# Two operand sums on VectorE, and a running sum on GpSimd: a change to the opening of a gated-mix kernel

## The chip, the cores and the metric

The kernel runs on one core of one Trainium2 chip. Its time is that of the whole launch, in device microseconds. Five engines work side by side, each with its own queue in program order: TensorE (PE, with its weight loads PEld), VectorE (DVE), ScalarE (ACT), GpSimd (POOL) and SyncE (SP). SyncE and GpSimd also issue DMA transfers, SyncE plain ones and GpSimd those that add to what is there (accumulating loads). Both kinds are moved by the same 16 DMA engines.

## What is computed

For x of 2048 rows and 512 columns:

```
q, k, v = split(x @ wqkv)                      # 32 heads of 16
phi(t)  = where(t > 0, t + 1, exp(t)) + 1e-6
kv = sum over rows of phi(k)^T v ;  z = sum over rows of phi(k)
a  = (phi(q) kv / (phi(q) z + 1e-6)) @ wo
b  = ((x @ w_gate) * (x @ w_up)) @ w_down
g  = sigmoid(sum(x * gate_w))
out = g * a + (1 - g) * b
```

All in float32, with EPS = 1e-6.

## The kernel before

**Three products for one.** TensorE multiplies in a shorter format, so that every float32 operand is split into a high part (a copy by ScalarE, `act`, line 58) and a low part (source less high part, by VectorE, `tt`, line 61). Each product is three matmuls (`mm3`, line 74): high by high, low by high, high by low. `split_late` (line 270) issues the high part at once and puts the low part on a list, `lows`, which `extras` (line 541) empties at the end of the same half step.

**Seven products for eight.** A product of two-by-two blocks is made in seven block products of sums of blocks (Strassen's scheme), numbered 1 to 7. `SUMS` (line 167) says which blocks of x make the operand of each: operand 3 is B1 - B2, 4 is A2 - A1, 1 is A1 + B2, 6 is A1 + B1, 7 is A2 + B2, while 2 is A1 and 5 is B2 alone. They are used in the order `UNIT` = 2, 3, 4, 1, 5, 6, 7.

**The two stages.** The main stage, from about 96 us on, makes q, the gate and up products and w_down. The first stage, which the change is about, makes k and v. It goes in steps of half steps:

- Steps 0 to 3: four lead tiles of 128 rows (tiles 8 to 11), their v by plain products (`plain`, line 299); their k came just before. The lead's x lies in `xa`.
- Steps 4 to 10: couples 4 and 5, seven block products each (s = 0 to 6), one of each couple in a step. Their operands are half-width sums of x (`sub`, lines 401 to 418).
- Steps 11 to 17 and 18 to 24: couples 0 and 1, then 2 and 3, with the full operands `xc` (operand 2 and 7 lie in `xa`, 3 and 5 in `xb`, which the lead and the half-width sums use before; 1, 4 and 6 have tiles of their own).

A product of block i of a couple adds to one of four PSUM banks Y, X, R, S (`couple`, line 429). Between the products `crit` moves results: m2 from Y by ScalarE, R = X - m2 by VectorE (called cR in the profile), v from Y, t, S, and so on. In a step, the first couple's product stands first, then the other couple's `crit`, then the second couple's product and the first couple's `crit`.

**phi and the sums over rows.** `phi_k` (line 302) makes exp and relu on ScalarE, joins them on VectorE, and adds the result and EPS to `zacc` on VectorE (line 307): the sum z. `phi_end` (line 310) adds EPS on ScalarE and frees a tile. `kv_add` multiplies phi(k) and v of a tile into `pkv` by 128 small matmuls; `gkv` gives the steps of the four groups of tiles. `z_sums` (line 611) reads `zacc` in slot 6 of the main stage.

**Operands of couples 0 to 3.** `op_load`, `op_add`, `op_turn` and `op_split` (lines 374 to 423) make them. For operands 2, 1, 5, 6 and 7: load a block into a DRAM scratch `xstage` (SyncE), add the other block there with an accumulating load (GpSimd), bring the sum to the low part's place in SBUF (`op_turn`, SyncE), split. For operands 3 and 4: load a block into two SBUF tiles `xo`, scale by -1 on ScalarE, add the other block with accumulating loads, split. `sub_load` and `sub_add` do the same for the half-width sums, in single `xo` tiles: seven loads at the start, then five accumulating loads.

**What sets the order.** Nothing is reordered: each engine runs its instructions as the program issues them. `plan(step, fn)` (line 334) puts a function at a half step; `AT` (line 40) holds the half steps, in the order of `UNIT` for the names with `gs` and `go`. So `goload` 3 for operand 2 means the second half of step 1. Negative numbers are run ahead of the lead. Within a half step, functions run in the order in which they were planned: phi first, then w_v's splits, then the operands, then the sums of weights and their splits.

**Work tiles.** `get` (line 187) takes the first of a list of 45 tiles, `put` (line 193) adds one at its end. An instruction that writes a tile handed out again waits until the last reader of its former content is done, and with it waits all that stands behind it in its queue.

**Weights of k and v.** w_k and w_v are loaded as four row blocks each (`raw_of`). `sum_make` (line 351) builds the sums of weight blocks on VectorE, `fac_split` (line 361) splits them, `split_v` (line 279) splits w_v's row blocks.

Of the kernel before, what the change touches and what calls it, by code (L numbers as in the profile page):

```python
# [1288 lines left out]
```

## Time and profile before

| What | Value |
| --- | --- |
| Three runs | 592.89, 591.58, 594.45 us (median 592.89) |
| Profiled execution | 593.48 us, its span 591.5 us |
| TensorE busy | 582.2 us (98%) |
| VectorE busy | 505.0 us (85%) |
| ScalarE busy | 418.3 us (71%) |
| GpSimd busy | 67.3 us (11%) |
| Mean granted TensorE clock | 0.996 |
| DMA | 99.29 MB, mean 168 GB/s |

In rows of the timeline the first number is the start in us from the span's beginning, the second the duration, then engine, line, operation, and output<-inputs; in square brackets stands the idle time of the engine just before and what ended it. A DMA row of SPq or POOL is the issue, not the transfer. Tile names are the program's: `xo` is a raw block of x or a sum being built, `xbh` and `xbl` are the high and low part in `xb`, `e` and `ph` belong to phi, `wvl` is w_v's low part, `c` with Y, X, R or S a couple's bank.

### The profile page before, as it was taken

Reading aid. Unit: us, or ns where it says so; the run is one execution under the profiler, and the core shown is the slowest. Engines: PE = TensorE matmul, PEld = TensorE weight load, DVE = VectorE, ACT = ScalarE, POOL = GpSimd, SP = SyncE. Lnnn points to the kernel's source line nnn. Section 1 sums busy time; section 2 is a strip of 40 time slices with the busy share of each in tenths; the row PEclk is TensorE's granted clock in tenths of the full one; section 3 lists DMA queues with packets and bytes.
Section 4 is the critical chain, followed back from the end, with each engine's and each line's share of the span. In section 5 each row is a group of like instructions: output and inputs, shape, how many; then the busy total and the mean of one; then the engine's idle time right before and its main releaser. Section 6 shows DMA issues by size and latency. Waiting matters only on the chain.

```text
span 591.5 us, 8699 instructions
## 1 busy us (share of the span) xinstructions
PE 582.2 (98%) x3047; PEld 474.6 (80%) x3047; DVE 505.0 (85%) x820; ACT 418.3 (71%) x755; POOL 67.3 (11%) x85
## 2 busy tenths in 40 slices
PE   8998999999999999999999999999999999999997
PEld 6785888777888888888888888888888888888885
DVE  7796687889698989998999976969899989889882
ACT  4588577879887878787974574887777677876300
POOL 0332000201111111111001100101101010100000
PEclk9999999999999999999999999999999999999999
DMA  8999674889797889878478356766847574631011
GB/s 280 227 271 235 205 169 148 196 209 222 183 251 178 213 203 242 192 183 212 109 219 218 115 133 188 150 139 149 188 106 162 150 159 116 134 81 35 1 74 69
DMA packets 45884, 99.29 MB, mean 168 GB/s; under 512 B 4384, under 2 KB 16928, under 8 KB 45728
## 3 DMA queue, kind: packets, MB, share of 16 engines
q0 software_dynamic: 11216, 37.49, 36.2%
q1 hardware_dynamic: 34336, 60.91, 30.0%
q8 instruction: 24, 0.39, 0.3%
q10 hardware_dynamic: 288, 0.33, 0.2%
q14 instruction: 20, 0.16, 0.1%
HBM read 87.43 MB, written 16.53 MB: 176 GB/s over the span
## 4 chain that ended last, share of the span: by engine, by line
PE 88%; ACT 4%; DMA 4%; DVE 2%; issue 1%; POOL 0%; SPq 0%; ACTq 0%; POOLq 0%
PE pdn L52 28%; PE bR L52 15%; PE bX L52 14%; PE bY L52 14%; PE bS L52 7%; PE pM L52 3%; DMA xo<-in_xp 2%; PE cR L52 2%; PE cY L52 2%; DMA wraw<-in_wqkv 2%; PE cX L52 1%; ACT e L58 1%; PE cS L52 1%; PE pkv L52 1%; ACT v L58 0%
## 5 line engine op out<-in xcount | busy, mean ns | idle before, releaser
L61 DVE TENSOR_TENSOR wcl<-wr,wch 128x512 fp32r<-128x512 f32 (+1 forms) x96 | 72.7, 772 | 5.2 <-ACT wch L58 5.2
L58 ACT ACTIVATE M<-pdn 128x512 f32<-128x512 f32 x84 | 49.9, 595 | 26.8 <-PE pdn L52 25.0
L52 PE MATMUL pdn<-hl,dh 128*128 128x512 f32 x176 | 68.5, 389 | 0.0
L52 PE MATMUL pdn<-hh,dh 128*128 128x512 f32 x176 | 68.5, 389 | 0.0
L52 PE MATMUL pdn<-hh,dl 128*128 128x512 f32 x176 | 68.5, 389 | 0.0
L58 ACT ACTIVATE wch<-wr 128x512 fp32r<-128x512 f32 (+1 forms) x96 | 66.7, 700 | 1.3 <-DMA wr<-in_wq_add 1.2
L61 DVE TENSOR_TENSOR M<-M,pdn 128x512 f32<-128x512 f32 x75 | 51.0, 681 | 13.9 <-PE pdn L52 13.7
L58 ACT ACTIVATE hh<-c 128x512 fp32r<-128x512 f32 x56 | 35.2, 629 | 37.0 <-DVE c L61 36.8
L85 POOL DMA_DIRECT2D wr<-in_wgu_add x28 | 24.3, 866 | 240.1 <-ACT wr L58 126.9
L52 PE MATMUL bX<-xbh,wch 128*128 128x512 f32 x128 | 49.8, 389 | 0.0
L52 PE MATMUL bX<-xbh,wcl 128*128 128x512 f32 x128 | 49.8, 389 | 0.0
L52 PE MATMUL bX<-xbl,wch 128*128 128x512 f32 x128 | 49.8, 389 | 0.0
L58 ACT ACTIVATE pdn<-M 128x512 f32<-128x512 f32 x61 | 35.9, 589 | 11.7 <-DVE M L61 11.7
L52 PEld LDWEIGHTS pdn<-hh,dh 128*128 128x128 f32 x176 | 33.0, 188 | 7.0
L52 PEld LDWEIGHTS pdn<-hl,dh 128*128 128x128 f32 x176 | 33.0, 188 | 7.0
L61 DVE TENSOR_TENSOR hl<-c,hh 128x512 fp32r<-128x512 f32 x56 | 38.3, 684 | 0.4
L52 PEld LDWEIGHTS pdn<-hh,dl 128*128 128x128 f32 x176 | 33.0, 188 | 6.8
L58 ACT ACTIVATE wr<-wr 128x512 f32<-128x512 f32 x64 | 36.7, 627 | 0.0
L61 DVE TENSOR_TENSOR dl<-dr,dh 128x512 fp32r<-128x512 f32 (+1 forms) x40 | 29.7, 764 | 2.3 <-ACT dh L58 2.1
L58 ACT ACTIVATE c<-bX 128x512 f32<-128x512 f32 x28 | 16.8, 600 | 20.0 <-DVE bS L61 20.0
L58 ACT ACTIVATE m<-bY 128x512 f32<-128x512 f32 x32 | 18.9, 591 | 16.5 <-PE bY L52 16.5
L58 ACT ACTIVATE dh<-dr 128x512 fp32r<-128x512 f32 (+1 forms) x40 | 27.1, 685 | 4.1 <-PE pdn L52 3.4
(265 smaller groups left out, 1597.3 us busy)
## 6 DMA issues: line engine op xcount, KB each, us to landing
wr<-in_wgu_add POOLq DMA_DIRECT2D x28, 640.0 KB, 6.4
wr<-in_wgu SPq DMA_DIRECT2D x28, 384.0 KB
dr<-in_wdn_add POOLq DMA_DIRECT2D x12, 640.0 KB, 6.9
dr<-in_wdn SPq DMA_DIRECT2D x12, 384.0 KB
xraw<-in_x SPq DMA_DIRECT2D x16, 256.0 KB
terms<-zq SPq DMA_DIRECT2D x16, 256.0 KB
zt<-terms SPq DMA_DIRECT2D x16, 256.0 KB
rb<-den SPq DMA_DIRECT2D x16, 256.0 KB
```

The costliest lines, as they stand in the source:

```text
L52: tc.keep_in_program_order(nc.tensor.matmul(*args, **kw))
L58: pin(nc.scalar.activation(dst, src, func, **kw))
L61: pin(nc.vector.tensor_tensor(dst, a, b, op=op))
L85: tc.keep_in_program_order(nc.gpsimd.dma_start(dst, src, accum_op=ALU.add))
```

## The change

Four edits, and new half steps in `AT`:

1. Operands 2 and 5 leave the DRAM scratch. `op_load(4)` now loads the blocks of operands 4 and 2 (A2 and A1), `op_load(3)` those of operands 3 and 5 (B1 and B2), each into four `xo` tiles with plain loads. `op_add` subtracts the one from the other on VectorE; the tiles of A1 and B2 are then split as operands 2 and 5 themselves. The scaling on ScalarE and the accumulating loads of operands 3 and 4 are gone.
2. `zacc` no longer gets phi and EPS from VectorE in `phi_k`; GpSimd adds the finished phi in `phi_end`.
3. In the couples, `phi_end` of all four tiles comes in s = 1 and 2 of the next pair of couples. Before, two of them came at s = 5 and two at s = 0 of the next.
4. The splits of w_v's first two row blocks are planned at -3, ahead of the sums of weights at -1; all four stood behind those sums on VectorE before.

In `AT`, by operand: loads of 4 at half step 5 (was 13), of 3 at 11 (was 9), of 1 at 7 (same), of 6 and 7 at 9 (were 11 and 9); splits of 2 at 11 (13), 3 at 19 (19), 4 at 10 (25), 1 at 23 (25), 5 at 25 (30), 6 at 27 (26), 7 at 28 (30). The last split of a weight sum is at 16 (18), and two groups of kv products come a step later (15 for 14, 28 for 27).

```diff
-'gwsplit': (-1, -1, 7, 9, 11, 13, 12, 14, 15, 18), 'goload': (3, 9, 13, 7, 11, 11, 9), 'goadd': (3, 14, 17, 9, 1, 13, 17), 'gosplit': (13, 19, 25, 25, 30, 26, 30)
+'gwsplit': (-1, -1, 7, 9, 11, 13, 12, 14, 15, 16), 'goload': (0, 11, 5, 7, 0, 9, 9), 'goadd': (0, 14, 8, 9, 0, 12, 14), 'gosplit': (11, 19, 10, 23, 25, 27, 28)
...
-'gkv': (6, 14, 22, 27)
+'gkv': (6, 15, 22, 28)
...
-'goturn': (7, 1, 5, 19, 19, 17, 20)
+'goturn': (0, 0, 0, 17, 0, 17, 20)
...
         stt(f32(ph), f32(e), 1.0, f32(ph), ALU.min, ALU.add)
-        stt(f32(zacc), f32(ph), EPS, f32(zacc), ALU.add, ALU.add)
         phi[t] = e, ph
...
         act(f32(e), f32(ph), AF.Identity, bias=epsc)
+        pin(nc.gpsimd.tensor_tensor(f32(zacc), f32(zacc), f32(e), op=ALU.add))
         put(ph)
...
-    xstage = {i: dram.tile([P, 2, CH], F32, name=f"xstage{i}") for i in (2, 1, 5, 6, 7)}
+    xstage = {i: dram.tile([P, 2, CH], F32, name=f"xstage{i}") for i in (1, 6, 7)}
+    WITH = {4: 2, 3: 5}
...
-        raw_op[i] = [get("xo") for _ in range(2)]
+        for k in (i, WITH[i]):
+            raw_op[k] = [get("xo") for _ in range(2)]
+            for b in range(2):
+                dma(f32(raw_op[k][b]), xp[0, SUMS[i][k != i]][:, b])
...
     def op_add(i):
+        for b in range(2):
+            if i in xstage:
                 dma_add(xstage[i][:, b], xp[0, SUMS[i][0]][:, b])
-            return
-        for b in range(2):
-            x_add(f32(raw_op[i][b]), 0, i, b)
+            else:
+                tt(f32(raw_op[i][b]), f32(raw_op[i][b]), f32(raw_op[WITH[i]][b]), ALU.subtract)
...
             elif s == 5:
-                phi_end(tb)
                 val_of(tb, bank["R"])
...
-        plan(-1, lambda k=k: split_v(k))
+        plan(-3 if k < 2 else -1, lambda k=k: split_v(k))
...
-                if s == 0 and ended:
+                if s in (1, 2) and ended:
                     phi_end(ended.pop(0))
...
-    later(1, lambda: phi_end(2))
-    later(1, lambda: phi_end(3))
+    for k, t in enumerate(ended):
+        later(k // 2, lambda t=t: phi_end(t))
```

More of the change, by code (lines that the diff above doesn't have):

```diff
@@ L39 @@
 STAYS = 1
-AT = {'gsload': (-1, -1, -1, -1, -1, -1, -1), 'gsadd': (1, 0, 1, -1, 1, -1, 1), 'gssplit': (1, 3, 5, 7, 11, 13, 9), 'gmake': (-1, -1, -1, -1, -1, -1, -1, 5, -1, -1), 'gwsplit': (-1, -1, 7, 9, 11, 13, 12, 14, 15, 18), 'goload': (3, 9, 13, 7, 11, 11, 9), 'goadd': (3, 14, 17, 9, 1, 13, 17), 'gosplit': (13, 19, 25, 25, 30, 26, 30), 'gwgu': (31, 33, 49, 31, 39), 'gw0': (41, 42, 44, 42, 45, 47), 'gkv': (6, 14, 22, 27), 'by': ((16383, 10920, 10922, 10922, 2730, 10990), (8191, 10922, 10922, 10920, 11946, 10922)), 'add': (2, 4), 'high': ((2, 3, 5), (2, 3, 5), (2, 3, 4)), 'low': ((4, 4, 5), (3, 5, 6), (4, 4, 5)), 'd': (7, 8, 8, 9, 9, 9, 9, 15), 'h': (7, 7, 8, 8, 9, 13, 14, 13, 14, 15, 14, 15, 16, 15, 16, 17, 16, 17, 19), 'q0': (8, 8, 10, 11, 15, 21, 23, 24, 26, 58, 11, 11), 'q1': (8, 9, 10, 13, 24, 30, 32, 34, 38, 42, 3, 6), 'wo': (70, 6, 10, 7), 'x': (3, 4, 8, 8, 12, 12), 'o': (-3, -1, 0, 5, 35, 36, 37, 39), 'xs': (36, 41, 40, 0, 1, 2, 4), 'plain': (4, 7, 8, 1, 6, 7, 12, 12, 2, 6), 'turn': (14, 2, 18, 1, 38, 4, 50, 6), 'first': (0, 4, 1, 4, 6, 6, 14, 3, 5, 17, 15, 16, 19, 21), 'goturn': (7, 1, 5, 19, 19, 17, 20), 'gxload': (25, 27, 28, 29, 31, 34, 37, 39, 41, 43, 47, 49, 51, 54, 56, 58), 'gxsum': (32, 33, 35, 37, 33, 36, 39, 41, 43, 51, 55, 56, 57, 59, 67, 69)}
@@ new lines @@
+AT = {'gsload': (-1, -1, -1, -1, -1, -1, -1), 'gsadd': (1, 0, 1, -1, 1, -1, 1), 'gssplit': (1, 3, 5, 7, 11, 13, 9), 'gmake': (-1, -1, -1, -1, -1, -1, -1, 5, -1, -1), 'gwsplit': (-1, -1, 7, 9, 11, 13, 12, 14, 15, 16), 'goload': (0, 11, 5, 7, 0, 9, 9), 'goadd': (0, 14, 8, 9, 0, 12, 14), 'gosplit': (11, 19, 10, 23, 25, 27, 28), 'gwgu': (31, 33, 49, 31, 39), 'gw0': (41, 42, 44, 42, 45, 47), 'gkv': (6, 15, 22, 28), 'by': ((16383, 10920, 10922, 10922, 2730, 10990), (8191, 10922, 10922, 10920, 11946, 10922)), 'add': (2, 4), 'high': ((2, 3, 5), (2, 3, 5), (2, 3, 4)), 'low': ((4, 4, 5), (3, 5, 6), (4, 4, 5)), 'd': (7, 8, 8, 9, 9, 9, 9, 15), 'h': (7, 7, 8, 8, 9, 13, 14, 13, 14, 15, 14, 15, 16, 15, 16, 17, 16, 17, 19), 'q0': (8, 8, 10, 11, 15, 21, 23, 24, 26, 58, 11, 11), 'q1': (8, 9, 10, 13, 24, 30, 32, 34, 38, 42, 3, 6), 'wo': (70, 6, 10, 7), 'x': (3, 4, 8, 8, 12, 12), 'o': (-3, -1, 0, 5, 35, 36, 37, 39), 'xs': (36, 41, 40, 0, 1, 2, 4), 'plain': (4, 7, 8, 1, 6, 7, 12, 12, 2, 6), 'turn': (14, 2, 18, 1, 38, 4, 50, 6), 'first': (0, 4, 1, 4, 6, 6, 14, 3, 5, 17, 15, 16, 19, 21), 'goturn': (0, 0, 0, 17, 0, 17, 20), 'gxload': (25, 27, 28, 29, 31, 34, 37, 39, 41, 43, 47, 49, 51, 54, 56, 58), 'gxsum': (32, 33, 35, 37, 33, 36, 39, 41, 43, 51, 55, 56, 57, 59, 67, 69)}
@@ L377, in op_load, with op_add @@
             return
-        raw_op[i] = [get("xo") for _ in range(2)]
+        for k in (i, WITH[i]):
+            raw_op[k] = [get("xo") for _ in range(2)]
+            for b in range(2):
+                dma(f32(raw_op[k][b]), xp[0, SUMS[i][k != i]][:, b])
+    def op_add(i):
         for b in range(2):
-            x_load(f32(raw_op[i][b]), 0, i, b)
-    def op_add(i):
-        if i in xstage:
-            for b in range(2):
+            if i in xstage:
                 dma_add(xstage[i][:, b], xp[0, SUMS[i][0]][:, b])
-            return
-        for b in range(2):
-            x_add(f32(raw_op[i][b]), 0, i, b)
+            else:
+                tt(f32(raw_op[i][b]), f32(raw_op[i][b]), f32(raw_op[WITH[i]][b]), ALU.subtract)
     ops_done = set()
@@ L477, in crit @@
                 phi_k(ta, bank["S"])
-        return product, crit, ta
+        return product, crit, (tb, ta)
     KV = (8, 9, 10, 11), (12, 14, 13, 15), (0, 4, 1, 5), (2, 6, 3, 7)
@@ L517, in gated_mix @@
         plan(G1["ssplit"][n], lambda i=i: sub_split(i))
-        plan(G1["oload"][n], lambda i=i: op_load(i))
         if i not in (2, 5):
+            plan(G1["oload"][n], lambda i=i: op_load(i))
             plan(G1["oadd"][n], lambda i=i: op_add(i))
@@ L576, in gated_mix @@
             extras(2 * step)
-            for h, (product, crit, ta) in enumerate(pair_of):
+            for h, (product, crit, _) in enumerate(pair_of):
                 product(s)
@@ L591, in gated_mix @@
             step += 1
-        ended = [ta for _, _, ta in pair_of]
+        ended = [ts[k] for k in range(2) for _, _, ts in pair_of]
         if two[0] != 2:
```

## The prediction

> **What bounds the kernel now.** I read the page's head first, then busy time by stretches of 10 us, then TensorE's own rows where a stretch is not full, and one piece of the chain of waits for the length of a step.
>
> ```profile
> span 591.5 us, 8699 instructions
> PE 582.2 (98%) x3047; PEld 474.6 (80%) x3047; DVE 505.0 (85%) x820; ACT 418.3 (71%) x755; POOL 67.3 (11%) x85
> ...
> PE   8998999999999999999999999999999999999997
> ...
> 30.00:40.00 10.00, 10.00 (x168) 8.20 (x167) 9.44 (x16) 10.00 (x21) 1.70 (x2) 1.00 0.92 312
> 40.00:50.00 10.00, 9.77 (x41) 7.25 (x40) 7.46 (x13) 6.43 (x13) 6.92 (x8) 1.00 0.96 157
> 50.00:60.00 10.00, 7.67 (x31) 5.75 (x30) 7.95 (x13) 9.99 (x20) 0.00 (x0) 0.91 0.94 251
> 60.00:70.00 10.00, 10.00 (x163) 8.07 (x162) 6.48 (x11) 4.42 (x9) 0.00 (x0) 0.92 0.82 289
> ```
>
> TensorE is the bound, and after the first 70 us it pauses only at the end, which the change doesn't touch. What can be won or lost lies ahead of that. Columns of a stretch: its length, then TensorE, weight loads, VectorE, ScalarE and GpSimd busy, granted clock, DMA share, GB/s. From 50 to 70 us there are a hole and a lower clock.
>
> ```profile
> 17.98 0.50 PE L52 MATMUL pv<-wvl,xah 128*128 128x512 f32 x1 [0.51 <-DVE wvl L61]
> 29.91 0.39 PE L52 MATMUL cY<-f2h,xbh 128*128 128x512 f32 x1
> 39.50 0.39 PE L52 MATMUL cR<-fh,xbh 128*128 128x512 f32 x1
> 50.09 0.39 PE L52 MATMUL cY<-f2h,xah 128*128 128x512 f32 x1
> 57.80 0.49 PE L52 MATMUL cY<-wvh,xc4h 128*128 128x512 f32 x1 [2.10 <-ACT xc4h L58]
> 58.52 0.79 PE L52 MATMUL cY<-wvh,xc4l 128*128 128x512 f32 x1 [0.23 <-DVE xc4l L61]
> 62.63 0.39 PE L52 MATMUL cR<-fh,xc1h 128*128 128x512 f32 x1
> ...
> 67.01 2.72 PE cX L52 x12
> ```
>
> The losses: 0.51 us before 17.98; 0.23 between 40 and 50 (10.00 less 9.77); 2.10 + 0.23 at operand 4 (57.8); and the clock, 10 x 0.09 + 10 x 0.08 = 1.7. Together 4.8 us, the most that the change can give. A step is 2.72 us, twelve matmuls 0.227 apart.
>
> **The change part by part.** *Low parts of w_v first.* VectorE works in order; only the first two low parts move up, the third stays where it was, behind the sums of weights.
>
> ```profile
> 17.24 2.49 DVE L61 TENSOR_TENSOR wvl<-wraw,wvh 128x512 fp32r<-128x512 f32 x4
> 32.34 0.69 DVE L64 SCALAR_TENSOR_TENSOR zacc<-ph,zacc 128x512 f32<-128x512 f32 x1
> 34.76 0.69 DVE L61 TENSOR_TENSOR sol<-xo,soh 128x512 fp32r<-128x512 f32 x1 [0.52 <-ACT soh L58]
> 38.38 0.69 DVE L61 TENSOR_TENSOR cR<-cX,m 128x512 f32<-128x512 f32 x1
> ...
> L64 DVE SCALAR_TENSOR_TENSOR zacc<-ph,zacc x16: 691/692/694, 21.6 to 98.3; 128x512 f32<-128x512 f32 x16
> L52 PE MATMUL pdn<-ones,zacc x32: 171/171/192, 106.9 to 107.2; 128*32 128x2 f32 x32
> ```
>
> Four are 0.60 apart (2.49 less 0.69, by three), so the third ends at 17.24 + 1.20 + 0.69 = 19.13 in both kernels. TensorE, not stopped at 17.47, wants it six matmuls later, at 18.8, and now stops there. Before, it came to it at 17.98 + 6 x 0.25 = 19.48. Gain 0.3, not 0.51.
>
> *Running sum on GpSimd.* Sixteen additions at 0.60 leave VectorE (9.6 us); only one of them (32.34) lies in a full stretch ahead of the cR at 38.38. What an add costs on GpSimd no row shows; nearest are a write of 512 columns and a one-input pass over 128.
>
> ```profile
> L992 POOL MEMSET kvm<- 128x512 f32 x1 | 0.9, 860 | 0.0
> L114 POOL TENSOR_SCALAR_AFFINE_SELECT bmask<-bmask 128x128 f32<-128x128 f32 x1 | 0.3, 340 | 0.1
> ...
> 17.66 5.80 POOL L85 DMA_DIRECT2D xo<-in_xp  x5 [15.83 <-DMA xo<-in_xp]
> 34.56 1.70 POOL L85 DMA_DIRECT2D xstage<-in_xp  x2 [11.10 <-DMA xstage<-in_xp]
> ```
>
> So between 0.86 and 4 x 0.34 = 1.36; I take 1.3, as it reads too. Each add waits for ScalarE's EPS pass; queued behind the fourth on GpSimd are the accumulating loads of operand 1 (34.56), and behind their landing SyncE's turn of it into SBUF. GpSimd stood 11.1 us there anyhow and the operand is wanted at 62.63, so this costs nothing; without that cover, 1.3 us each. The last four adds take 5.2 us after 98.3 and end near 104, ahead of the z product at 106.9.
>
> *EPS later.* Sixteen passes stay sixteen, 0.61 apart; the four that stood ahead of xc4h on ScalarE come one to two steps later: 2.4 us out of that queue. The kv products move a step with them, at the same cost.
>
> *Two sums by VectorE.* Gone: four scalings on ScalarE, four accumulating loads of 256 KB, two staging loads and two turns of 512 KB. New: four plain loads of 256 KB and four subtractions of 0.60.
>
> ```profile
> 26.29 0.63 ACT L58 ACTIVATE xbh<-xo 128x512 fp32r<-128x512 f32 x1 [3.02 <-DMA xo<-in_xp]
> 28.88 0.64 ACT L58 ACTIVATE xbh<-xo 128x512 fp32r<-128x512 f32 x1
> 32.96 0.64 ACT L58 ACTIVATE m<-cY 128x512 f32<-128x512 f32 x1
> 39.69 1.21 ACT L58 ACTIVATE xo<-xo 128x512 f32<-128x512 f32 x2
> 45.55 1.15 ACT L58 ACTIVATE xo<-xo 128x512 f32<-128x512 f32 x2
> 49.61 0.73 ACT L58 ACTIVATE e<-ph,epsc 128x512 f32<-128x512 f32 x1
> 56.02 0.72 ACT L58 ACTIVATE e<-ph,epsc 128x512 f32<-128x512 f32 x1
> 57.13 1.14 ACT L58 ACTIVATE xc4h<-xo 128x512 fp32r<-128x512 f32 x2
> ```
>
> With 4 x 0.52 = 2.1 of scalings and 2.4 of EPS (first and last of the four shown) out of ScalarE's queue, and operand 4's split moved from step 12 to step 5, the wait at 57.8 goes and its slow clock with it. The 0.23 goes too: the last factor split moves up a step. Taking the 62.63 row against 50.09 plus three steps of 2.72, this is 62.63 - 58.25 = **4.4 us off**.
>
> Now the price. Ahead of couple 5's cR (38.38, step 6) VectorE gets two subtractions, two low parts of operand 4 and two of operand 2: six, less one running sum, 5 x 0.60 = 3.0, of which the 0.52 gap at 34.76 takes some: cR would run from 40.8 to 41.5. TensorE wants it at 39.50 - 0.3 = 39.2: **a new stall of 2.2 us**, even if nothing else is late.
>
> *When the loads run*, the step that I rely on most. Work tiles are handed out first in, first out. Counted off that list, operand 4's load at step 5 first gets the tile of w_v's third row block, which is free when its low part has been read, at 19.13. SyncE waits for that, then issues four loads, three staging loads and operand 3's loads, 3.5 MB, with the first packets near 20.3. Before, SyncE stood from 13.7 to 27.15 and its queue was empty in this time; exactly there run the five accumulating loads of the half-width sums, from GpSimd's queue.
>
> ```profile
> 12.79 0.95 SPq L82 DMA_DIRECT2D xstage<-in_xp  x1
> 27.15 0.34 SPq L82 DMA_DIRECT2D xal<-xstage  x1
> ...
> q1 hardware_dynamic: 1943, 2.53, 99.3%
> ...
> q0 software_dynamic: 1260, 1.22, 100.3%
> ...
> q0 software_dynamic: 363, 0.66, 97.8%
> ...
> q0 software_dynamic: 216, 0.40, 54.2%
> q1 hardware_dynamic: 216, 0.81, 53.4%
> ```
>
> These are DMA queues (packets, MB) from 8 to 16 us (SyncE's alone), 20 to 28 and 44 to 48 (GpSimd's alone), 53 to 57 (both). In 4 us GpSimd's queue moves 363 packets alone and 216 beside the other: 0.6 of its rate; SyncE's then moves 0.2 MB/us, so 3.5 MB last to 37.8. Operand 3's half-width sum lands at 26.27; the 6.0 us of that behind 20.3 become 10.0: 30.3, four late. Operand 4's follows 0.26 MB / (1.22 MB / 8 us) = 1.7 later, 28.0, and becomes 20.3 + 7.7 / 0.6 = 33.1. Bounds for the first: 26.3, if the queues don't mind each other; 26.3 + 8 = 34.3, if GpSimd's stands still while SyncE's moves its first 2.5 MB (the 8 to 16 row). I take 30.3, from the only row with both.
>
> ScalarE in order (0.48 a copy from PSUM, 0.52 a cast, 0.61 EPS): xbh at 30.3, then v of the second lead tile, done 31.45. Its bank is wanted by couple 5's first product, 29.91 before, 29.6 now: TensorE stops 1.8 us. xbh of operand 4 at 33.1 instead of 28.88 pushes all behind it by 4.2: m from 32.96 to 37.2, done 37.8; couple 4's third product, ready at 35.6, stops 2.3. Couple 5's cR is done at 45.4; its product, 39.50 before, starts 5.9 late, this stall 1.6. Nothing waits from there on; step 10 ends at 55.0 instead of 50.1 (4.9 later), so the row at 62.63 comes **0.5 us late**: 4.9 lost, 4.4 won. The stalls may slow the clock as the 2.10 did; what that costs behind the first two is hidden by the wait that follows, behind the third not: 0 to 1.7, I take 0.7. So +1.2 us on the profiled execution's 593.48 (its span and 2 us): 594.7. The median of the runs, 592.89, is 0.6 below that execution: **594.1**.
>
> **The rivals.** *B, the queues pass one another.* For: SyncE's loads might start later than I count. Against: 216 and 216. The 2.2 us stall then stands alone: cR's product at 41.5, step 10 ends 51.0, the 62.63 row comes at 59.1, 3.5 early, or 1.8 if the stall slows the clock: 589.4 to 591.1.
>
> *C, all removed and no new wait.* VectorE would have to hide its five extra pieces; against it, its 9.44 of 10 us between 30 and 40. 592.9 - 4.8 = 588.1.
>
> *D, slower: GpSimd's adds hold VectorE up.* For: GpSimd ran nothing with two inputs, so the trace can't exclude it. Place: steps 3 to 6, with two adds in VectorE's full stretch ahead of cR; price 2 x 1.3 = 2.6 on the forecast's walk and some 0.5 for the four adds of steps 12 and 13: 597.2. It decides once a 0.69 piece takes over 1.3 beside an add. [...]
>
> **How the numbers follow.** Forecast 0.44, B 0.28, C 0.13, D 0.15. Half a per cent, 3.0 us, is about what a measurement of this kernel tells from no change: under 589.9 is faster, over 595.9 slower. The forecast's own range is 592.0 to 598.1 (first sum at 34.3, four later than taken); a quarter of it is slower, 0.11, the rest same, 0.33. Half of B is faster, half same. Faster 0.14 + 0.13 = 0.27; slower 0.11 + 0.15 = 0.26; same 0.33 + 0.14 = 0.47. The range from 588.6 to 598.2 leaves out most of C and the upper part of D.
>
> **What would show it.** Right: no TensorE wait at 57 and clock 1.00; ScalarE waiting 6 us and more for xo where it waited 3.02; TensorE waits near 30 (v), 36 (m) and 44 (cR); packets of both queues between 20 and 30; SyncE's first load after the half-width sums at 19 to 20. Wrong: xbh at 26.3 (B); no wait at cR (C); VectorE's pieces at twice 0.69 beside an add, or an add far over 1.4 us (D).

## The result and the profile after

The changed kernel takes 601.21 us (median of 4 runs, 599.88 to 602.88) against 593.07 us (4 runs, 591.58 to 594.45): a ratio of 1.0133, interval 1.0103 to 1.0163. It is slower by 8.1 us. The forecast was 594.1 with a range of 588.6 to 598.2; the time lies above all of it. The profiled execution after took 602.88 us, its span 600.9 us.

The page of the kernel after: its head, the busy time, TensorE in 40 slices, and the group of the new GpSimd adds (count, then busy time and mean ns of one, then idle time before them and what ended it).

```profile
span 600.9 us, 8722 instructions
...
PE 582.1 (97%) x3047; PEld 474.4 (79%) x3047; DVE 506.3 (84%) x808; ACT 416.7 (69%) x751; POOL 88.0 (15%) x97
...
PE   8857999999999999999999999999999999999997
...
L312 POOL TENSOR_TENSOR zacc<-zacc,e 128x512 f32<-128x512 f32 x16 | 26.2, 1637 | 52.3 <-ACT e L58 51.6
```

TensorE is busy for as long as before (582.1 us for 582.2), so that the 9.4 us that the span grew are time in which it waits. The digits place them: the second to fourth slice, 15 to 60 us, read 8, 5, 7 where they read 9, 9, 8. The same stretches of 10 us as before, in the same columns:

```profile
30.00:40.00 10.00, 3.26 (x8) 2.59 (x9) 2.39 (x4) 4.43 (x9) 1.29 (x1) 0.74 0.86 187
40.00:50.00 10.00, 8.87 (x157) 6.74 (x156) 9.45 (x14) 9.47 (x20) 7.68 (x8) 0.92 0.34 52
```

From 30 to 40 us *no* engine is busy for half the time, so none of them is the bound there; what they wait for has to come from outside, and only the DMA share (0.86) is high. (The clock of 0.74 is a mean. In the same view by half microseconds it is 0.50 from 35 to 41.5 us and 1.00 ahead of 34.5 and behind 42; until 36.74 TensorE waits; its matmuls then start 0.43 us apart until 41.17 and 0.23 apart from 41.85 on, so that at most half of the other 4.9 us is lost by it, 2.4.) TensorE's waits after, from its timeline:

```profile
18.75 0.51 PE L52 MATMUL pv<-wvl,xah 128*128 128x512 f32 x1 [1.00 <-DVE wvl L61]
36.74 0.79 PE L52 MATMUL cY<-f2h,xbh 128*128 128x512 f32 x1 [7.27 <-ACT v L58]
46.88 0.50 PE L52 MATMUL cY<-wvh,xbh 128*128 128x512 f32 x1 [0.91 <-ACT m L58]
48.75 0.50 PE L52 MATMUL cR<-fh,xbh 128*128 128x512 f32 x1 [0.22 <-DVE cR L61]
52.36 0.50 PE L52 MATMUL cR<-fh,xbh 128*128 128x512 f32 x1 [1.96 <-DVE cR L61]
72.87 0.51 PE L52 MATMUL cR<-fh,xc1h 128*128 128x512 f32 x1 [0.86 <-DVE cR L61]
...
115.38 0.47 PE L52 MATMUL bS<-xah,wch 128*128 128x512 f32 x1 [0.48 <-DVE bS L61]
```

The waits at 57.80 and 58.52 are gone, as wanted. In their place stand three that the forecast named (v, m, cR) and two that it did not (72.87, 115.38). The largest is 7.27 us for ScalarE's v. ScalarE's own row and SyncE's issues say why v was late:

```profile
35.57 0.63 ACT L58 ACTIVATE xbh<-xo 128x512 fp32r<-128x512 f32 x1 [12.74 <-DMA xo<-in_xp]
...
7.69 12.88 SPq L82 DMA_DIRECT2D xo<-in_xp  x11
20.61 2.19 SPq L82 DMA_DIRECT2D xstage<-in_xp  x3
22.90 4.27 SPq L82 DMA_DIRECT2D xo<-in_xp  x4
```

Ahead of v in ScalarE's queue stands the split of operand 3's half-width sum, and that sum landed at 35.57 instead of 26.29. SyncE's queue stood until about 20 us (the 11 are the seven half-width loads and the first four of the new ones) and then let go all of the new loads at once, just when the accumulating loads run.

How late TensorE is at a given place is better read from the start of *the same matmul* in two traces than from the lengths of waits, since a wait is also longer for an engine that came early. The starts below are the first matmul of each name (for wvl, the third); each cell of a run is its start less the start before, so that a plus is late.

| Matmul | start before | after | e1 | e3 | e5 | e8 | e9 | e10 | e11 | e12 |
| --- | --- | --- | --- | --- | --- | --- | --- | --- | --- | --- |
| pv<-wvl (third) | 19.48 | -0.73 | -0.70 | -0.67 | -0.01 | +0.07 | -0.68 | -0.06 | -0.99 | +0.53 |
| cX<-wkh,xbh | 31.27 | +8.20 | -0.52 | -0.54 | +0.16 | +1.84 | -0.56 | +0.11 | -0.83 | +2.54 |
| cR<-fh,soh | 43.58 | +12.99 | +6.05 | -0.10 | +5.62 | +7.85 | -0.10 | +1.52 | +1.73 | +5.49 |
| cY<-f2h,xah | 50.09 | +12.21 | +4.99 | -0.88 | +4.54 | +7.09 | -0.24 | +1.40 | +1.01 | +9.70 |
| cR<-fh,xc1h | 62.63 | +7.86 | +0.62 | -0.69 | +0.17 | +2.72 | -2.41 | -2.72 | -3.34 | +5.83 |
| cS<-fh,xah | 72.29 | +9.05 | +0.62 | -0.50 | +0.18 | +3.94 | -2.24 | -2.05 | +0.32 | +5.84 |
| pdn<-ones,zacc | 106.93 | +9.99 | +1.56 | +0.45 | +0.41 | +4.90 | -2.03 | -1.84 | +1.26 | +6.79 |

The column "after" is the whole story in seven numbers: 0.7 us earlier at w_v, 13.7 lost by 43.58, 0.8 regained by 50.09, 4.35 won back between 50.09 and 62.63 (the removed wait), 2.1 lost again up to 107 us, and little from there on. The other columns are the experiments.

### The profile page after: what moved, and what is told of

The parts are those of the page before. It is cut to its first block, busy times and chain, and to the rows that moved or that the text cites. A ratio compares the mean times of both kernels' runs of the same rounds, so it can differ in the third digit from the quotient of the medians.

```text
span 600.9 us, 8722 instructions
## 1 busy us (share of the span) xinstructions
PE 582.1 (97%) x3047; PEld 474.4 (79%) x3047; DVE 506.3 (84%) x808; ACT 416.7 (69%) x751; POOL 88.0 (15%) x97
## 4 chain that ended last, share of the span: by engine, by line
PE 84%; DMA 6%; DVE 4%; ACT 3%; issue 2%; SPq 1%; POOL 0%; DVEq 0%; ACTq 0%; POOLq 0%
PE pdn L52 28%; PE bY L52 14%; PE bR L52 14%; PE bX L52 14%; PE bS L52 7%; DMA xo<-in_xp 4%; PE pM L52 3%; PE cR L52 1%; DMA wraw<-in_wqkv 1%; PE cX L52 1%; PE cY L52 1%; ACT e L58 1%; DMA xraw<-in_x 1%; ACT ph L58 1%; DVE junk L289 1%
## 5 line engine op out<-in xcount | busy, mean ns | idle before, releaser
L61 DVE TENSOR_TENSOR M<-M,pdn 128x512 f32<-128x512 f32 x75 | 51.2, 683 | 13.8 <-PE pdn L52 13.7
L312 POOL TENSOR_TENSOR zacc<-zacc,e 128x512 f32<-128x512 f32 x16 | 26.2, 1637 | 52.3 <-ACT e L58 51.6
```

The costliest lines, as they stand in the source:

```text
L61: pin(nc.vector.tensor_tensor(dst, a, b, op=op))
L312: pin(nc.gpsimd.tensor_tensor(f32(zacc), f32(zacc), f32(e), op=ALU.add))
```

## The experiments

Three theories could each make part of the 8 us:

1. *Displaced loads.* SyncE's 3.5 MB, let go at 20 us, starve GpSimd's accumulating loads.
2. *GpSimd's adds and VectorE shut each other out.* In the profile after, two subtractions take 2.38 us beside the add at 43.77 and two low parts at 46.80, beside none, 1.28.
3. *VectorE's crowd.* The pieces that edit 1 brings forward delay the second cR.

### The loads

**e1, late loads.** Operand 4's and 2's loads are planned at half step 8 and get tiles that TensorE leaves at about 27 us; by SyncE's order the later loads follow them, all but one staging copy (12.77 us). Nothing else is changed.

```diff
-    def get(name):
-        k = spare.pop(0)
+    def get(name, k=None):
+        k = spare.pop(0 if k is None else spare.index(k))
...
-            raw_op[k] = [get("xo") for _ in range(2)]
+            raw_op[k] = [get("xo", {4: (22, 23), 2: (24, 25)}[k][b] if i == 4 else None) for b in range(2)]
...
-'goload': (0, 11, 5, 7, 0, 9, 9)
+'goload': (0, 11, 8, 7, 0, 9, 9)
```

> The changed kernel, but operand 4's four loads are issued at half step 8 into tiles of w_v's first two row blocks, which TensorE frees near 27 us, so that all loads but one staging load run behind the accumulating loads of the half-width sums; all else as in the changed kernel (601.2 us). Theory 1 (loads displaced into the time of the accumulating loads): operand 3's half-width sum lands near 26 to 27 instead of 35.6, the 7.27 us wait is gone, 590 to 594 us. Theory 2 (GpSimd's adds and VectorE shut each other out): 598 to 601, VectorE's pieces still lengthened. Theory 3 (VectorE crowded ahead of the second cR): the 7.27 wait may go but the cR stall grows, 596 to 599.

Measured: 595.01 us (5 runs, 594.72 to 596.14), ratio 1.0030 [1.0016, 1.0043]. ScalarE's row for operand 3's sum, TensorE's remaining long wait and the stretch around it:

```profile
27.01 0.63 ACT L58 ACTIVATE xbh<-xo 128x512 fp32r<-128x512 f32 x1 [4.14 <-DMA xo<-in_xp]
...
43.81 0.50 PE L52 MATMUL cR<-fh,xbh 128*128 128x512 f32 x1 [1.96 <-DVE cR L61]
...
40.00:50.00 10.00, 7.84 (x26) 5.99 (x27) 9.76 (x17) 4.75 (x10) 1.57 (x2) 0.83 1.06 228
```

The sum lands at 27.01 and the 7.27 us wait is gone: 6.2 of the 8.1 us were the loads. The wait for cR stays, 1.96 us to the hundredth, and VectorE is busy 9.76 of 10 us around it. So theory 1 is the larger part, and something else is left.

**e4, the sums alone.** Edit 1 with edits 2, 3 and 4 undone (VectorE keeps the running sum, `phi_end` and `split_v` are as before).

```diff
+        stt(f32(zacc), f32(ph), EPS, f32(zacc), ALU.add, ALU.add)
...
-        pin(nc.gpsimd.tensor_tensor(f32(zacc), f32(zacc), f32(e), op=ALU.add))
...
+                phi_end(tb)
...
-        plan(-3 if k < 2 else -1, lambda k=k: split_v(k))
+        plan(-1, lambda k=k: split_v(k))
```

> Edit 1 alone (two sums by VectorE, with the half steps of the changed kernel for operands and factor splits); running sum on VectorE, EPS passes and kv products at their places of before, all w_v splits at -1. Theory 1: 599 to 602. Theory 2: 591 to 595. Theory 3: 596 to 600, the cR stall at 2 us or more without GpSimd's adds.

Measured: 600.53 us (4 runs, 599.58 to 604.03), ratio 1.0131 [1.0098, 1.0163], and operand 3's sum as late as in the whole change:

```profile
35.80 0.63 ACT L58 ACTIVATE xbh<-xo 128x512 fp32r<-128x512 f32 x1 [13.01 <-DMA xo<-in_xp]
```

Edit 1 by itself makes the loss. The other three, on top of it, add 0.7 us, inside the spread of either; below it turns out that this is a loss and a gain.

**e8, staging late.** Only operand 4's and 2's 1 MB stay beside the accumulating loads; the three staging copies and operand 3's and 5's loads come after (SyncE issues the staging at 27.60 us).

```diff
-'goload': (0, 11, 5, 7, 0, 9, 9), 'goadd': (0, 14, 8, 9, 0, 12, 14)
+'goload': (0, 10, 5, 11, 0, 11, 11), 'goadd': (0, 14, 8, 13, 0, 13, 14)
```

> The changed kernel with operand 3's loads and the three staging loads of 512 KB put behind the four loads of operand 4 and 2, operand 3's behind the tiles that TensorE frees near 27: only 1 MB in packets of 2 KB runs beside the accumulating loads until then. If the queues share by bytes and rate (0.6 of the rate, as in the prediction): operand 3's half-width sum lands at 28 to 29 and the wait at couple 5's first product falls from 7.27 to under 1 us; 594 to 597. If they alternate by packets, so that the staging loads' packets of 32 KB hold it most: the same landing of 28 to 30, and the 5 us between this and the changed kernel's 35.6 are the staging loads' share. If the number of loads doesn't matter but that they run at all: 33 or later.

Measured: 598.55 us (3 runs, 597.32 to 598.59), ratio 1.0081 [1.0054, 1.0107]. Operand 3's sum:

```profile
30.44 0.63 ACT L58 ACTIVATE xbh<-xo 128x512 fp32r<-128x512 f32 x1 [6.80 <-DMA xo<-in_xp]
```

4.2 late instead of 9.3, so the 1 MB explains less than half of the delay. The landing is a little behind the 28 to 30 expected; the wait at couple 5's first product (1.29 us for under 1) and the time (594 to 597) came out above what was expected.

**e12, staging beside.** The counterpart: one operand tile holds SyncE's queue as in the change, behind it come the three staging copies, and the other three tiles only when TensorE has left theirs. The splits are late as in e6 (below), which is its comparison.

```diff
-        for k in (i, WITH[i]):
-            raw_op[k] = [get("xo") for _ in range(2)]
-            for b in range(2):
+        raw_op[i], raw_op[WITH[i]] = [], []
+        order = [(k, b) for k in (i, WITH[i]) for b in range(2)]
+
+        def some(part, tiles):
+            for (k, b), tile in zip(part, tiles):
+                raw_op[k].append(get("xo", tile))
                 dma(f32(raw_op[k][b]), xp[0, SUMS[i][k != i]][:, b])
+
+        if i == 3:
+            some(order, (None,) * 4)
+        else:
+            some(order[:1], (None,))
+            plan(10, lambda: some(order[1:], (23, 24, 25)))
...
-'goadd': (0, 14, 8, 9, 0, 12, 14), 'gosplit': (11, 19, 10, 23, 25, 27, 28)
+'goadd': (0, 17, 14, 9, 0, 12, 14), 'gosplit': (16, 20, 18, 23, 25, 27, 28)
```

> Of the loads that the change moves, only 1.75 MB stand beside the accumulating loads of the half-width sums: one of operand 4's four tiles, whose wait still holds SyncE's queue until about 19 to 20 us, and behind it the three staging copies of 0.5 MB, which move in packets of 32 KB; the other three tiles come when TensorE has left theirs, near 27 us. The running sum is on GpSimd and the splits are late, as in the run with late loads and late splits (595.39 us). It is the counterpart of the run with 1 MB of operand tiles beside the accumulating loads and the staging late, where operand 3's sum landed at 30.44 us, 4.2 late. If GpSimd's queue loses by the byte, 1.75 MB cost 1.75 times that: a landing near 33.6 and a time near 600. If each packet of SyncE costs it a turn, however long, 48 packets of 32 KB and 128 of 2 KB are fewer than 512 of 2 KB and cost less: a landing near 28 and a time near 596. A landing above 33.6 would say that the long packets cost more than their bytes.

Measured: 600.44 us (4 runs, 599.72 to 601.02), ratio 1.0115 [1.0093, 1.0136]: 5 us above e6, and near the 600 of the rule by the byte. The landing, which tells more directly what the loads did, is at 31.15 and lies between the two numbers expected (28 by the packet, 33.6 by the byte). ScalarE's row, and the DMA queues (packets, MB, share of the engines' time) from 24 to 28 us:

```profile
31.15 0.63 ACT L58 ACTIVATE xbh<-xo 128x512 fp32r<-128x512 f32 x1 [7.06 <-DMA xo<-in_xp]
...
q1 hardware_dynamic: 103, 1.53, 100.5%
q0 software_dynamic: 117, 0.11, 18.5%
```

In these four microseconds GpSimd's queue (q0) moves 117 packets, 29 a microsecond. How many it moves alone, and beside other kinds of packets, is read from the same view of four stretches: before, 20 to 26 us; after, 31 to 35 and 25 to 29; and e2 (next), 29 to 32.

```profile
q0 software_dynamic: 889, 0.86, 95.8%
```

```profile
q0 software_dynamic: 390, 0.38, 58.7%
q1 hardware_dynamic: 385, 0.70, 53.6%
...
q1 hardware_dynamic: 132, 1.57, 97.2%
q0 software_dynamic: 129, 0.13, 20.4%
```

```profile
q1 hardware_dynamic: 90, 1.31, 104.3%
q0 software_dynamic: 86, 0.09, 17.5%
```

Alone: 889 in 6 us, 148 a microsecond. Beside SyncE's operand tiles (0.70 MB in 385, most of 2 KB): 97, that is 0.66. Beside the staging copies (in after's stretch all but 0.1 of the 1.57 MB in 45 packets, so 32 KB each): 32 in after and 29 in e2 and e12, that is 0.2. In all of these rows the two queues' counts are alike, to 14% in e12 and to 5% in the others, the 39 to 64 packets of under 512 bytes in each stretch, most of them SyncE's, counted in. In e8 they are not: from 24 to 28 us SyncE's queue moved 451 (0.82 MB) and GpSimd's 322, 80 a microsecond or 0.54. So neither of the two rules in e12's expectation holds alone. Alike counts look like two queues that take turns packet for packet, long or short, and a landing between the two rules agrees with that; but it is the author's reading of the counts: no turn is seen in a trace, and e8's row does not fit it. What the runs show is the rate left to GpSimd's queue: 0.54 to 0.66 beside packets of 2 KB, 0.2 beside packets of 32 KB. GpSimd's adds are no rival for this delay: e4 has none of them, and its sum lands as late (35.80).

**e2, the sum on VectorE.** Edit 2 undone alone.

```diff
         stt(f32(ph), f32(e), 1.0, f32(ph), ALU.min, ALU.add)
+        stt(f32(zacc), f32(ph), EPS, f32(zacc), ALU.add, ALU.add)
...
-        pin(nc.gpsimd.tensor_tensor(f32(zacc), f32(zacc), f32(e), op=ALU.add))
```

> The changed kernel with the running sum back on VectorE in phi_k (edit 2 undone alone). Theory 1: the wait for operand 3's sum stays, 599 to 601. Theory 2: 593 to 596, pieces of 0.69 throughout. Theory 3: one more piece ahead of cR, 601 to 602.

Measured: 598.87 us (4 runs, 598.23 to 601.15), ratio 1.0099 [1.0076, 1.0122]. It looks like 2.3 us for edit 2, but the trace does not allow that reading:

```profile
29.84 0.63 ACT L58 ACTIVATE xbh<-xo 128x512 fp32r<-128x512 f32 x1 [5.62 <-DMA xo<-in_xp]
35.77 0.63 ACT L58 ACTIVATE xbh<-xo 128x512 fp32r<-128x512 f32 x1 [3.23 <-DMA xo<-in_xp]
```

In this execution SyncE's queue was let go 1.4 us later (staging issued at 22.06, not 20.61) and the long packets ran from 29 to 32 us, when operand 3's sum had just landed. So it escaped them, and operand 4's sum met them instead. The collision depends on a microsecond of the start; edit 2 has to be priced without it.

### GpSimd's adds

**e3, without the sums.** Edit 1 undone alone: operands 2 to 5 are made as before, with edits 2, 3 and 4.

```diff
-    xstage = {i: dram.tile([P, 2, CH], F32, name=f"xstage{i}") for i in (1, 6, 7)}
+    xstage = {i: dram.tile([P, 2, CH], F32, name=f"xstage{i}") for i in (2, 1, 5, 6, 7)}
...
-                tt(f32(raw_op[i][b]), f32(raw_op[i][b]), f32(raw_op[WITH[i]][b]), ALU.subtract)
+            x_add(f32(raw_op[i][b]), 0, i, b)
```

> The changed kernel with edit 1 undone alone: operands 2 to 5 made as before, at the half steps of before; running sum on GpSimd, late EPS passes and early low parts of w_v kept. Theory 1: operand 3's sum lands near 26, 590 to 593, the stall of operand 4 near 57 shorter than 2.1 as ScalarE has four EPS passes fewer ahead of it. Theory 2: 597 to 600. Theory 3: 590 to 593, as the six pieces are gone.

Measured: 594.98 us (10 runs, 593.33 to 597.07), ratio 1.0031 [1.0015, 1.0047], between the ranges that the theories gave. Operand 3's sum lands at 25.54 and up to 98 us TensorE is 0.5 to 0.9 us ahead of the kernel before; then it falls behind. GpSimd, VectorE and TensorE there:

```profile
97.06 6.83 POOL L312 TENSOR_TENSOR zacc<-zacc,e 128x512 f32<-128x512 f32 x4 [11.16 <-ACT e L58]
...
99.27 1.77 DVE L289 SCALAR_TENSOR_TENSOR junk<-xraw,gw 128x512 f32<-128x512 f32 x1
...
103.27 1.18 DVE L64 SCALAR_TENSOR_TENSOR phq<-ex,phq 128x512 f32<-128x512 f32 x1
...
105.82 0.47 PE L52 MATMUL bS<-xah,wch 128*128 128x512 f32 x1 [0.51 <-DVE bS L61]
126.29 0.50 PE L52 MATMUL bR<-xc6h,wch 128*128 128x512 f32 x1 [0.71 <-DVE t L61]
```

Four adds take 1.71 us each, VectorE's piece of 0.68 takes 1.77, and TensorE waits twice for VectorE.

**e9, EPS and w_v.** e3 with the running sum back on VectorE, so that only edits 3 and 4 are left.

```diff
+        stt(f32(zacc), f32(ph), EPS, f32(zacc), ALU.add, ALU.add)
...
-        pin(nc.gpsimd.tensor_tensor(f32(zacc), f32(zacc), f32(e), op=ALU.add))
```

> Only the third and fourth edit (EPS later, two low parts of w_v first); no sums of operands by VectorE, and the running sum stays on VectorE. It asks what held the run without the sums (edits two to four) at 594.98 us, 1.8 above the kernel before. There the trace shows four GpSimd adds of 1.7 us each at 97 to 104 us, VectorE's pieces of 0.68 us at 1.77, and TensorE waits of 0.51 (bS, 105.82) and 0.71 us (bR after t, 126.29). If GpSimd's adds and VectorE shut each other out (theory 2), those waits go with them and the time is at or under the kernel before: about 592.5 us, since the third low part of w_v lets TensorE on 0.5 us earlier; VectorE's pieces of 0.68 us stay 0.68 at 97 to 104. If EPS later or the order of w_v costs by itself, it stays at 594 to 595.

Measured: 591.67 us (12 runs, 590.73 to 592.95), ratio 0.9979 [0.9963, 0.9995]. The same piece of VectorE, and what is left of the wait for operand 4:

```profile
97.76 0.68 DVE L289 SCALAR_TENSOR_TENSOR junk<-xraw,gw 128x512 f32<-128x512 f32 x1
...
56.21 0.49 PE L52 MATMUL cY<-wvh,xc4h 128*128 128x512 f32 x1 [0.75 <-ACT xc4h L58]
```

The piece is 0.68 again, the waits at bS and t are gone, and the time falls by 3.3 us against e3. By the table 0.7 of the difference of 2.5 us at 106.93 arises after 72.29, at the pieces shown; the other 1.7 is there at 62.63 already. The two come to operand 4's first product together (56.10 in e3, after a wait of 1.26, and 56.21). From there e3's low parts xc4l take 0.80 and 0.98 us instead of 0.69, beside two adds at 55.07 (2.96 us for the two), and TensorE waits 0.4 us more for them; and e3's clock is 0.50 from 58.2 to 61.5 us, where e9's stays at 1.00, which costs by estimate half of the 2.9 us in which TensorE then works, 1.5. So edit 2 costs at both places by VectorE's pieces that are longer beside the adds, but most of what it costs at the first is the clock of this execution. Edits 3 and 4 together are a gain of 1.4 us, since the wait for xc4h goes from 2.10 to 0.75 us and the clock behind it, 0.91 and 0.92 from 50 to 70 us before, stays at 1.00.

### VectorE's crowd

Three runs on the base of e1 tried to clear what was left there. e5 puts the running sum back on VectorE (the diff of e2). e6 moves the sums and splits of operands 2, 3 and 4 later. e7 does both.

```diff
-'goadd': (0, 14, 8, 9, 0, 12, 14), 'gosplit': (11, 19, 10, 23, 25, 27, 28)
+'goadd': (0, 17, 14, 9, 0, 12, 14), 'gosplit': (16, 20, 18, 23, 25, 27, 28)
```

> e1_late_loads with the running sum back on VectorE in phi_k: the price of GpSimd's adds without the displaced loads. Theory 2 (GpSimd's adds and VectorE's pieces with two SBUF inputs shut each other out): e1's 2.38 us for two subtractions falls to 1.29, its second cR comes about 1 us earlier, and the 0.5 us wait at the first bS near 107 goes; 1.5 to 2.5 us less than e1 (595.0). If the shutting out costs nothing where TensorE waits: 0 to 0.5 less, or 0.6 more for the piece that VectorE has more.

> e1_late_loads with the subtraction and the split of operand 4 and the split of operand 2 moved behind the second cR (half steps 14, 18 and 16 for 8, 10 and 11), those of operand 3 to 17 and 20. Theory 3 (VectorE crowded ahead of the second cR): the waits of 0.94 and 1.96 us go, 3 us less than e1: 591.5 to 592.5. If GpSimd's adds cause them: they stay at 1 us or more, 594 to 595.

> All three: loads behind the accumulating ones, running sum on VectorE, splits behind the second cR. If the three causes add up: 589 to 590.5, that is faster than the kernel before (593.2), with no TensorE wait over 0.5 us between 15 and 62 us and clock 1.00. If another wait takes their place: 592 to 594.

Measured: 595.28 us (12 runs, 594.21 to 595.99), 595.39 (12, 593.76 to 598.42) and 595.07 (12, 593.40 to 596.99); ratios 1.0029 [1.0015, 1.0043], 1.0035 [1.0020, 1.0050] and 1.0031 [1.0014, 1.0047]. None moved, and none came to what theories 2 and 3 gave it (1.5 to 2.5 us under e1, 591.5 to 592.5, 589 to 590.5), though each does what it says. In e5 the wait for cR stays. In e7 it is gone, and a longer one stands further on, with what VectorE did just ahead of it:

```profile
43.40 0.80 PE L52 MATMUL cR<-fh,xbh 128*128 128x512 f32 x1 [1.94 <-DVE cR L61]
```

```profile
49.13 1.28 DVE L61 TENSOR_TENSOR xo<-xo 128x512 f32<-128x512 f32 x2
50.33 1.29 DVE L61 TENSOR_TENSOR xc4l<-xo,xc4h 128x512 fp32r<-128x512 f32 x2
51.53 0.69 DVE L61 TENSOR_TENSOR cS<-t,cX 128x512 f32<-128x512 f32 x1
...
52.28 0.79 PE L52 MATMUL cS<-fh,soh 128*128 128x512 f32 x1 [3.19 <-DVE cS L61]
```

Four pieces of 0.6 us, moved away from the second cR, now stand ahead of the second cS, which TensorE wants just as much (e6 the same: 2.50 us at 54.14). So these runs do not refute theory 3; they moved the crowd to the next place where it hurts. What was needed is a place where VectorE waits anyhow.

**e10, sums in gaps.** The base is e5. VectorE's pause between a couple's cS and ScalarE's ph (1.15 and 1.21 us before) takes the two sums, by a list that `phi_k` empties between its two ScalarE passes and its VectorE piece; operand 2's tiles are freed only after operand 4's sum. The splits of operands 2 and 3 are where the kernel before has them, and operand 4's comes behind its sum (half step 21).

```diff
+        while between:
+            between.pop()()
         stt(f32(ph), f32(e), 1.0, f32(ph), ALU.min, ALU.add)
...
-            plan(G1["oadd"][n], lambda i=i: op_add(i))
+            plan(G1["oadd"][n], (lambda i=i: between.append(lambda: op_add(i))) if i in WITH else (lambda i=i: op_add(i)))
...
-'goadd': (0, 14, 8, 9, 0, 12, 14), 'gosplit': (11, 19, 10, 23, 25, 27, 28)
+'goadd': (0, 16, 18, 9, 0, 12, 14), 'gosplit': (13, 19, 21, 23, 25, 27, 28)
```

> The run with late loads and the sum on VectorE, with the four sums of operands 3 and 4 put where VectorE waits for ScalarE's ph anyway (idle 1.15 and 1.21 us at 45.7 and 49.8 us in the trace of before) and operand 2's and 3's splits where the kernel before has them, so that VectorE's order up to the second cS is that of before. If VectorE's crowd ahead of the second cR and the second cS is what remains (theory 3), TensorE's waits for cR (1.95), t and cS (2.5 to 3.2) go, xc4h no longer ends a wait of 2.10 near 57 us and the half clock after it goes: span 591.7 to 592.8 less about 2 to 4, that is about 589 to 591 us of span and 591 to 593 us of time. If something else holds it (the loads beside other transfers, what lies outside the span), it stays near 595.

Measured: 590.88 us (12 runs, 589.29 to 592.06), ratio 0.9955 [0.9941, 0.9969]: faster than the kernel before by 2.2 us, and 10.3 below the change. Time and median span (588.75) lie just under what theory 3 expected. Of the 2.2 us, edits 3 and 4 have 1.4 alone, as e9 shows; edit 1 in the gaps adds 0.8, and in the two profiled executions it adds nothing (-2.03 and -1.84 at 106.93). VectorE's gaps hold the sums:

```profile
46.62 1.28 DVE L61 TENSOR_TENSOR xo<-xo 128x512 f32<-128x512 f32 x2
47.92 0.69 DVE L64 SCALAR_TENSOR_TENSOR ph<-e,ph 128x512 f32<-128x512 f32 x1
...
49.85 1.28 DVE L61 TENSOR_TENSOR xo<-xo 128x512 f32<-128x512 f32 x2
51.09 0.69 DVE L64 SCALAR_TENSOR_TENSOR ph<-e,ph 128x512 f32<-128x512 f32 x1
```

ph follows with no idle time noted ahead of it, where VectorE waited 1.15 and 1.21 us before. No wait for cR above 0.3 us is left, one of 0.66 stands at the second cS, and none near 57 us. Theory 3 is shown, since e7, which only moved the pieces further on, gained nothing: with the pieces in gaps, edit 1 costs 1.5 us by 43.58 (most of it an m wait of 1.03) where e5 has 5.6, and wins back 4.2 by 62.63.

**e11, gaps with GpSimd.** The same with the running sum on GpSimd: all four edits.

```diff
-        stt(f32(zacc), f32(ph), EPS, f32(zacc), ALU.add, ALU.add)
...
+        pin(nc.gpsimd.tensor_tensor(f32(zacc), f32(zacc), f32(e), op=ALU.add))
```

> The same places for the sums, but the running sum on GpSimd as in the change: all four edits, with the loads late and the sums in the gaps. Theory 2 gives it 1 to 1.5 us more than the same kernel with the sum on VectorE, by TensorE's waits at bS (0.5) and after t (0.3 to 0.7) between 98 and 128 us, and the pieces of 0.68 us of VectorE in the gaps at over 1 us beside GpSimd's adds. Without that theory the two come out alike.

Measured: 592.79 us (12 runs, 591.33 to 594.87), ratio 1.0003 [0.9987, 1.0019]: 1.9 us above e10. Theory 2 gave 1 to 1.5. The waits expected near 98 to 128 us came in part (0.50 at bS, none after t). The larger part lies where it was not expected:

```profile
58.45 6.36 POOL L316 TENSOR_TENSOR zacc<-zacc,e 128x512 f32<-128x512 f32 x4 [16.58 <-ACT e L58]
...
59.47 2.51 DVE L61 TENSOR_TENSOR xbl<-xo,xbh 128x512 fp32r<-128x512 f32 x2 [0.85 <-ACT xbh L58]
61.91 0.69 DVE L61 TENSOR_TENSOR cR<-cX,m 128x512 f32<-128x512 f32 x1
...
62.65 0.50 PE L52 MATMUL cR<-fh,xc1h 128*128 128x512 f32 x1 [1.84 <-DVE cR L61]
```

Two low parts ahead of couple 1's cR take 2.51 us instead of the 1.29 that they take in e10, and TensorE waits 1.84 instead of 0.23. The sums in the gaps stayed at 1.28 and 1.29: no GpSimd add ran then (one ended at 36.87, the next began at 58.45).

## Why the prediction was wrong

The sign was called even (0.27 faster, 0.26 slower) and the size was missed by 7 us. Step by step:

*When the loads run* is one of two steps that failed. Its mechanism was right: the tile, the wait, the 3.5 MB let go near 20 us, the victims and their order. The term mis-sized is the rate of GpSimd's queue beside SyncE's. It was taken as 0.6 from the one row with both, where SyncE's packets have 3.8 KB in the mean (0.81 MB in 216). Beside 2 KB packets 0.54 to 0.66 was measured, close to it; beside the staging copies' 32 KB packets 0.2. The half-width sum landed at 35.57, not 30.3, and not even within the bound of 34.3, which let GpSimd's queue stand still for SyncE's first 2.5 MB only. From there the working does follow: the v stop was 7.27 instead of 1.8, 5.5 more for 5.3 of later landing. The clock was misplaced: 0.7 was put behind the third stop, but it fell in the first. It cost up to 2.4 us there, ahead of the waits for m and cR, and how much of that these waits would have hidden, as the forecast assumed, is not shown.

*Two sums by VectorE* was right in its gain and wrong in its price. "4.4 us off" was measured as 12.21 less 7.86, 4.35. The new stall at cR was put at 2.2 where nothing else is late; e1 shows 1.96 and e5 1.94. But the stall is not the whole price. e1, whose sum lands at 27.01, is 4.99 us late at the product at 50.09, where rival B, with the same stall and no collision, had step 10 end 0.9 late (51.0), or 2.6 with the clock. Beside cR's 1.96 + 0.22 stand m stops of 0.88 and 0.94 and a clock of 0.83 over 10 us, 1.7. So without any collision the removed wait is paid for in full: e1 is 0.62 late at the 62.63 product and e5 0.17, where B had 1.8 to 3.5 early. Rival C, all removed and no new wait (588.1), has its counterpart in e10 (590.88).

The forecast had TensorE 4.9 us late at the end of step 10, of which 0.9 is B's and 4.0 the loads'. Measured, it is 12.2: 5.0 as in e1, and 7.2 more by the loads. The crowd was too small by 4.1 us, the loads by 3.2.

*Running sum on GpSimd* was wrong. Taken at 1.3 an add, the shortest add is 1.29, but the mean is 1637 ns; the last four took 6.84 instead of 5.2 us. It "costs nothing" for the queue behind it, which is so, but not for VectorE. Rival D's condition, a 0.69 piece over 1.3 beside an add, is met (1.77), and the price it put on these waits, 2.6, lies between e11 less e10 (1.9) and e3 less e9 (3.3, with the clock). But two more pairs differ in this edit alone and show no such price: e1 less e5 is -0.3 us and e6 less e7 0.3, in median span 0.45 and 0.8. So the price depends on what stands beside the adds, and no single number is shown. D and the forecast were treated as alternatives; both happened. In the kernel after, the rows are:

```profile
43.30 2.38 DVE L61 TENSOR_TENSOR xo<-xo 128x512 f32<-128x512 f32 x2
...
68.66 6.38 POOL L312 TENSOR_TENSOR zacc<-zacc,e 128x512 f32<-128x512 f32 x4 [18.54 <-ACT e L58]
...
69.68 2.53 DVE L61 TENSOR_TENSOR xbl<-xo,xbh 128x512 fp32r<-128x512 f32 x2 [0.84 <-ACT xbh L58]
72.13 0.69 DVE L61 TENSOR_TENSOR cR<-cX,m 128x512 f32<-128x512 f32 x1
```

D's place was only half right: the two subtractions at 43.30 are in steps 3 to 6, where it put them, but of the 2.1 us lost between the products at 62.63 and 106.93 most is at couple 1's cR (0.86) and at bS (0.48), by adds that edit 3 had put behind one another.

*Low parts of w_v first* was right in the place: the first wait is gone, and TensorE stops at the third low part instead, 1.00 us, longer than the 0.51 before. It is still 0.73 us earlier at that matmul (0.3 forecast); a wait read alone would have told the opposite. The size is not shown, as the lead's own start varies: the traces with this edit lie from 0.99 us earlier to 0.66 later there, and e4, without it, is 0.49 earlier.

*EPS later* was right: xc4h no longer waits behind four EPS passes, and with edit 4 it makes e9's 1.4 us. Without any operand sum on VectorE, e9 wins 2.2 us between the products at 50.09 and 62.63, half of the 4.4 that the forecast gave to both edits together.

In one line: forecast +1.2 on the profiled span, measured +9.4. By the table, 7.3 more were lost up to the product at 50.09, 0.05 less was won back, and 2.1 were lost from there to 107 us, most of it beside GpSimd's adds; 0.6 was regained after that, and the 0.7 that the forecast held for the clock is already in the first. 7.3 + 0.05 + 2.1 - 0.6 - 0.7 is the 8.2 between them.

## What to carry to other kernels

When a change moves a transfer, ask not only how many bytes it puts beside a critical one, but in packets of what length: here a queue with 1 KB packets moved 148 a microsecond alone, 80 to 97 beside packets of 2 KB, and 29 to 32 beside copies in packets of 32 KB, four fifths of its rate gone. Work moved to an engine that has spare time on the average needs its gap named on the timeline (the same sums, with the splits that go with them, cost 4.1 us more by 43.58 in VectorE's full stretch than between cS and ph). To see what a wait costs, compare the start of the same matmul in both traces.

## What the runs showed of the hardware

- **GpSimd and VectorE.** Beside GpSimd's adds, which have two inputs from SBUF, VectorE pieces with both inputs in SBUF took longer: 1.77 us for 0.68 (junk, e3 at 99.27 and 100.97), 2.38 to 2.86 for 1.29 (pairs, after at 43.30, 69.68 and 72.73); one in e3, junk at 98.66, stayed at 0.68. Four adds took 1.71 each (6.83 in e3 from 97.06, 6.84 after from 106.62), where the shortest takes 1.29. Pieces with one input in PSUM kept their time: cR 0.69 at 72.13 in the middle of the adds (after) and at 61.91 (e11), t 0.68 at 102.67 (e3).
- **The clock.** The granted clock fell after some long stops and not after others: e1 with 1.96 us at cR reads 0.83 from 40 to 50 us, e7 with 3.19 at cS 0.66 from 50 to 60, e11 with 1.84 at cR 0.83 from 60 to 70, the kernel before with 2.10 reads 0.91 and 0.92; but e8 with 1.95 at cR and e6 with 2.50 at cS stay at 1.00. What decides it is not shown, and the length of the stop alone is not it. By half microseconds, before and after, it is 0.50 or 1.00, with a mean between them only where it changes. It stays at 0.50 for 3.4 us (before from 58.3, e1 from 44.5, e3 from 58.2), 6.8 (after from 34.8, e7 from 51.1) or 10.3 (e4, 32.9 to 43.2); the means of the stretches agree (e1 0.83 over 10 us, e3 0.91 and 0.92 over two of 10, e7 0.66 over 10, e4 0.83 over 30). With matmuls 0.43 us apart instead of 0.23 (before, after, e4 and e7), 3.4 us of it lose by estimate 1.6 to 1.7 where TensorE works all through them, and less where it waits in them.
- **Outside the span.** Time less span is 1.9 us in the mean for the kernel before and for the change, and 1.7 to 2.1 in most runs, but 2.1 to 2.5 in the five that have both the operand sums and the running sum on VectorE (e2, e4, e5, e7, e10; 2.54 in e5). Of the 1.8 us by which e5's median time is over the kernel before, 0.6 is therefore not in its span (592.75 for 591.65). The cause is not shown.
